# Attention and routed experts on one core: whole value tiles, scores on 64x32 tiles, sums from the exponentials, one comparison per rank block

## The chip, the cores and the metric

The kernel runs on 1 NeuronCore of one Trainium2 chip. The metric is the device time of one execution in microseconds (us), the median of several runs. The engines are TensorE (PE; its weight loads are PEld in the profile), VectorE (DVE), ScalarE (ACT), GpSimd (POOL) and SyncE (SP, which here only issues DMAs), and the core has 16 DMA engines. Each engine takes its instructions in program order and waits on semaphores.

## What is computed

Eight batches, 8 heads, 512 local and 32 global tokens, head size 64, all in fp32. A local query sees the 32 global keys and the local keys within 32 positions; a global query sees all 544 keys. Over the result, seen as 544 tokens of 512 numbers, a router takes the 128 tokens with the highest score in each batch, and these pass through two dense layers with a gate.

```python
k_all = np.concatenate([k_g, k_l], axis=2)
v_all = np.concatenate([v_g, v_l], axis=2)
out_g = np.matmul(sm(scale * np.matmul(q_g, k_all.transpose(0, 1, 3, 2))), v_all)
mask = np.abs(pos[:, None] - pos[None, :]) <= 32
s_ll = np.where(mask, scale * np.matmul(q_l, k_l.transpose(0, 1, 3, 2)), -1e9)
s_lg = scale * np.matmul(q_l, k_g.transpose(0, 1, 3, 2))
out_l = np.matmul(sm(np.concatenate([s_lg, s_ll], axis=-1)), np.concatenate([v_g, v_l], axis=2))
# sm(s): e = exp(s - max(s)); e / (sum(e) + 1e-9)
...
scores = np.einsum('bsd,d->bs', x, w_gate)          # x: tokens, 544 x 512
top_idx = np.argpartition(-scores[b], 128)[:128]
ye = np.maximum(x[b, top_idx] @ w1, 0.0) @ w2       # 512 -> 1024 -> 512
out[b, top_idx] = x[b, top_idx] + sigmoid(scores[b, top_idx])[:, None] * ye
```

## The kernel before

**Steps.** The attention runs in 64 steps: batch b, half of the heads hq (4 heads), and a quarter t of the local queries (128 queries). Four steps make a group, eight a batch. One loop writes the program order of PE, DVE, ACT and POOL by hand: iteration i issues the scores of step i+2, the products with the values of step i-1, the transposes of step i, the softmax of step i+1 and the normalising of step i-1. The order of DMA issues on SyncE is left to the framework.

**Scores.** `scores` computes for 32 queries of one chunk the products with their window of 128 keys (chunk before, own chunk, globals, chunk after; the keys lie in `k_t` in such an order that a window is one access pattern). Two heads share 128 partitions (64 numbers each), so `spread_q` writes the queries into `qbd` with zeros in the other head's half: a stationary operand of 128x64 gives both heads at once. A step is 8 such products into one PSUM bank `s_ps` of two. Each fp32 product is two matmul records in the trace, a transpose one.

**Softmax.** For each 128x128 block, four a step, VectorE adds the mask and takes the negated maximum (L238), and ScalarE takes the exponential in place (L242). PE transposes the four blocks (L250), ScalarE copies them out (`turned`, L255). `attend_mm` (L273) multiplies by the value tile `v_t`, whose rows have a 65th column of ones, so that the sum of the exponentials comes out as a 65th column. `attend_out` takes that sum, its reciprocal and scales (L284, L286, L291), once each step.

**Value tiles.** A group needs two (`half` 0 and 1). A tile holds 8 windows of 128 rows; rows 64 to 95 are the globals in each. `load_v` (L150) loads partitions 0 to 63 and 96 to 127 in two DMAs, and `fill_v` (L157) copies the globals from `vg_t` into partitions 64 to 95 on POOL. There are three buffers.

**Globals.** Once a group the `g_` functions do the same for the 32 global queries of 4 heads over all 544 keys, in the two banks `big`.

**Tokens to experts.** `finish` writes a step's 128 tokens to HBM and scores them (L302). When a batch is done, `chain` runs its links over the following steps: `spread` turns the 544 scores into a row on all partitions, `rank` (five times) counts for a block of 128 tokens how many tokens go before each, `onehot` compares the ranks with 0 to 127, `gather` turns that into indices on PE and fetches the tokens by an indirect DMA. Ties go by position: `rank` compares with `>=` over the tokens up to the own block (L406) and with `>` over the rest (L408), with weights `side_w` that cut the own block in a triangle. The experts' work of earlier batches (`ffn1_pair` L520, `ffn2` L536) is cut into pieces and put between the steps by `run_fill`; batches go in the groups (0), (1,2), (3,4), (5,6), (7). Its result goes back by an indirect DMA (L543).

Of the kernel before, what the change touches and what calls it, by code (L numbers as in the profile page):

```python
# [72 lines left out]
def kernel(ctx, tc, qT, kT, qgT, vw, vgw, w1, w2, wg, const, outs, cap):  # L73
# [24 lines left out]
    half = cst.tile([P, 2], FP32, name="half")  # L98
    nc.vector.memset(half, 0.0)
    for i in range(2):  # L100
        nc.vector.memset(half[D * i:D * i + D, i:i + 1], 1.0)
# [2 lines left out]
    nc.scalar.activation(out=warm, in_=half, func=AF.Exp)
    # Weights of a comparison by position: 0 and 1 at the tokens' own block, 1 in all blocks on the side that counts.
    side_w = cst.tile([P, SL + 2 * P], FP32, name="side_w")
    nc.gpsimd.memset(side_w[:, P:P + SL], 1.0)
# [3 lines left out]

    qbd = [cst.tile([P, 2, NC, 2, 32], FP32, name=f"qbd{i}") for i in range(2)]

    def load(b, hq):
# [4 lines left out]
        if b == 0 and hq == 0:  # L119
            nc.sync.dma_start(out=q_t[:, :, 0:P], in_=qT[b, :, prs, 0:P])  # L120
            nc.sync.dma_start(out=k_t[:, :, 0:2 * P], in_=kT[b, :, prs, 0:2 * P])
            nc.sync.dma_start(out=cs[:, 0:3 * P], in_=const[:, 0:3 * P])
            nc.sync.dma_start(out=q_t[:, :, P:SL], in_=qT[b, :, prs, P:SL])
            nc.sync.dma_start(out=k_t[:, :, 2 * P:KW], in_=kT[b, :, prs, 2 * P:KW])
        else:
            nc.sync.dma_start(out=q_t, in_=qT[b, :, prs])
            nc.sync.dma_start(out=k_t, in_=kT[b, :, prs])
# [734 lines left out]
```

## Time and profile before

| | us |
|---|---|
| median of 3 runs | 355.31 |
| lowest and highest | 353.08, 362.15 |
| span of the profiled execution, first to last instruction | 353.1 |

The page gives no other time for the profiled execution than its span; the lowest of the three runs lies beside it. In the prediction's rows, "busy" is the time in which an engine executed something, "xN" the number of instructions, "idle before" the time the engine stood still just before them, followed by what ended it. Rows in order of time begin with the start and the length in us. PEclk is the granted clock as a share of full speed, "DMA share" the busy share of the 16 DMA engines. L-numbers are lines of the kernel before.

### The profile page before, as it was taken

How to read it: one execution, taken by the hardware profiler on the slowest of the kernel's cores; microseconds unless marked ns; L12 is line 12 of the kernel's file. 1: busy time of each engine (PE TensorE's matmuls, PEld its weight loads, DVE VectorE, ACT ScalarE, POOL GpSimd, SP SyncE). 2: the span in 40 equal slices, each digit the busy share in tenths (PEclk: the TensorE clock that was granted, in tenths of full speed). 3: DMA queues.
4: the chain of work that ended last, by engine and by line, in shares of the span. 5: the costliest groups of instructions: out<-in, count | busy, mean ns of one | idle time of the engine just before them, and what ended most of it. 6: DMA issues, size and time to landing. Idle time of an engine off the chain costs nothing.

```text
span 353.1 us, 12662 instructions
## 1 busy us (share of the span) xinstructions
PE 307.8 (87%) x5112; PEld 244.1 (69%) x5112; DVE 261.5 (74%) x1142; ACT 172.0 (49%) x445; POOL 137.7 (39%) x91
## 2 busy tenths in 40 slices
PE   6766798678996969679899999999899999999993
PEld 2654576466674757467688887768698877699882
DVE  1334767898669996997689977998699799995222
ACT  2455737457662645245653663455655445322020
POOL 1326647708754633404395205154356112211111
PEclk9899889989999889969999999999999999999999
DMA  7999989987998593938986777659784841311000
GB/s 201 257 208 320 264 275 300 279 247 218 319 248 291 123 299 71 253 121 219 274 183 219 193 226 193 187 169 255 230 229 141 218 96 62 135 58 32 30 30 30
DMA packets 23033, 67.99 MB, mean 193 GB/s; under 512 B 7360, under 2 KB 9280, under 8 KB 19904
## 3 DMA queue, kind: packets, MB, share of 16 engines
q1 hardware_dynamic: 21696, 63.00, 63.9%
q0 software_dynamic: 1280, 4.20, 3.9%
q8 instruction: 40, 0.66, 0.8%
q14 instruction: 17, 0.14, 0.1%
HBM read 56.18 MB, written 11.01 MB: 190 GB/s over the span
## 4 chain that ended last, share of the span: by engine, by line
PE 35%; DVE 19%; issue 12%; POOL 3%; DMA 3%; ACT 1%; POOLq 0%; DVEq 0%; ACTq 0%; SPq 0%
PE s_ps L222 7%; PE m_ps L520 5%; DVE junk L406 5%; PE o_ps L273 4%; PE m_ps L536 4%; PE t_ps L250 4%; DVE p_t L238 3%; DVE junk L302 3%; DVE junk L408 2%; PE big L361 2%; PE big L318 2%; DVE x L291 1%; DMA xe<-out_dram,ix 1%; POOL qbd L145 1%; DMA xg<-out_dram 1%
## 5 line engine op out<-in xcount | busy, mean ns | idle before, releaser
L242 ACT ACTIVATE p_t<-p_t,nb 128x128 f32<-128x128 f32 x256 | 81.9, 393 | 77.4 <-DVE nb L238 77.2
L222 PE MATMUL s_ps<-k_t,qbd 128*64 128x128 f32 x1024 | 77.0, 296 | 27.2 <-issue 12.8
L222 PEld LDWEIGHTS s_ps<-k_t,qbd 128*64 128x64 f32 x1024 | 60.4, 147 | 42.8 <-issue 19.2
L157 POOL TENSOR_SCALAR v_t<-vg_t 32x2080 f32<-32x2080 f32 x32 | 65.1, 2035 | 54.5 <-issue 16.5
L238 DVE CUSTOM_DVE_ANT_0 p_t<-s_ps,cs 128x128 f32<-128x128 f32 x256 | 58.5, 284 | 3.2 <-PE s_ps L222 3.2
L273 PE MATMUL o_ps<-v_t,pt 128*32 128x65 f32 x2048 | 45.9, 229 | 7.1 <-issue 4.5
L255 ACT COPY pt<-t_ps 128x512 f32<-128x512 f32 x64 | 36.7, 574 | 25.5 <-PE t_ps L250 25.1
L273 PEld LDWEIGHTS o_ps<-v_t,pt 128*32 128x32 f32 x2048 | 34.5, 113 | 18.3 <-issue 13.0
L250 PE MATMUL t_ps<-cs,p_t 128*128 128x128 f32 x256 | 44.2, 298 | 0.0
L145 POOL TENSOR_SCALAR qbd<-q_t,half 128x1024 f32<-128x1024 f32 x29 | 34.6, 1201 | 14.5 <-DMA q_t<-in_qT_dram 8.7
L438 POOL DMA_INDIRECT xe<-out_dram,ix x8 | 8.7, 1087 | 69.1 <-issue 49.1
L406 DVE SCALAR_TENSOR_TENSOR junk<-r,sc,side_w 128x128 f32<-128x128 f32 (+4 forms) x40 | 34.7, 868 | 1.0 <-ACT r L394 0.3
L250 PEld LDWEIGHTS t_ps<-cs,p_t 128*128 128x128 f32 x256 | 28.2, 146 | 6.0 <-issue 0.9
L302 DVE CUSTOM_DVE_ANT_0 junk<-x,wgb 128x512 f32<-128x512 f32 x32 | 29.2, 913 | 0.8
L408 DVE SCALAR_TENSOR_TENSOR junk<-r,sc,side_w 128x544 f32<-128x544 f32 (+4 forms) x40 | 28.1, 704 | 1.6
L291 DVE TENSOR_TENSOR x<-o_ps,rec 128x256 f32<-128x256 f32 x64 | 27.2, 424 | 2.2
L284 DVE TENSOR_SCALAR den<-o_ps 128x4 f32<-128x4 f32 x64 | 10.0, 157 | 21.9 <-PE o_ps L273 13.1
L543 POOL DMA_INDIRECT out_dram<-xe,ix x8 | 8.2, 1023 | 36.1 <-DVE xe L541 28.8
L520 PE MATMUL m_ps<-xTh,w1h 128*128 128x256 f32 x80 | 21.2, 297 | 0.0
L238 DVE DVE_READ_ACCUMULATOR2_ANT nb<- 128x1 f32 x256 | 20.8, 81 | 0.0
L536 PE MATMUL m_ps<-w2h,hTh 128*128 128x512 f32 x48 | 20.7, 431 | 0.0
L520 PE MATMUL m_ps<-xTh,w1l 128*128 128x256 f32 x80 | 19.9, 282 | 0.0
(133 smaller groups left out, 485.0 us busy)
## 6 DMA issues: line engine op xcount, KB each, us to landing
v_t<-in_vw_dram SPq DMA_DIRECT2D x32, 520.0 KB
k_t<-in_kT_dram SPq DMA_DIRECT2D x15, 832.0 KB
v_t<-in_vw_dram SPq DMA_DIRECT2D x32, 260.0 KB
out_dram<-x SPq DMA_DIRECT2D x32, 256.0 KB
q_t<-in_qT_dram SPq DMA_DIRECT2D x15, 512.0 KB
ws<-in_w_dram SPq DMA_DIRECT2D x8, 512.0 KB
k_t<-in_kT_dram SPq DMA_DIRECT2D x1, 576.0 KB
vg_t<-in_vgw_dram SPq DMA_DIRECT2D x16, 32.5 KB
```

The lines of the kernel that those rows point to most:

```text
L145: nc.gpsimd.tensor_scalar(out=out, in0=in_, scalar1=h, scalar2=0.0, op0=ALU.mult, op1=ALU.add)
L157: nc.gpsimd.tensor_scalar(out=v_t[64:96], in0=bass.AP(tensor=src.tensor, offset=src.offset, ap=[src.ap[0], [0, 8], [1, 4 * VD]]), scalar1= ...
L222: nc.tensor.matmul(out=s_ps[D * par:D * par + D, pr, uu, :], lhsT=z[:, pr, c].rearrange("p a k -> p (a k)"), rhs=window(k_t[:, pr, k0:k0 + ...
L238: nc.vector.tensor_tensor_reduce(out=p_t[:, pr, uu, :], in0=s_ps[:, pr, uu, :], in1=m, op0=ALU.add, op1=ALU.min, scale=-0.125, scalar=BIG, ...
L242: nc.scalar.activation(out=p_t[:, pr, uu, :], in_=p_t[:, pr, uu, :], func=AF.Exp, scale=-1.0, bias=nb[:, pr, uu:uu + 1])
L250: nc.tensor.transpose(t_ps[:, pr, uu, :], p_t[:, pr, uu, :], ident)
L255: nc.scalar.copy(out=pt, in_=t_ps)
L273: nc.tensor.matmul(out=o_ps[32 * j:32 * j + 32, 2 * pr + h, :], lhsT=pt[:, pr, j // 2, x0:x0 + 32], rhs=v_t[:, j % 2, 2 * (t % 2) + j // 2 ...
L302: nc.vector.tensor_tensor_reduce(out=junk[:n, 0:DM], in0=xf, in1=wgb[:n], op0=ALU.mult, op1=ALU.add, scale=1.0, scalar=0.0, accum_out=dst,)
L406: nc.vector.scalar_tensor_tensor(out=junk[:n, 0:hi], in0=r[:n, 0:hi], scalar=s, in1=side_w[:n, P + SL - lo:P + SL - lo + hi], op0=ALU.is_g ...
L408: nc.vector.scalar_tensor_tensor(out=junk[:n, lo:ST], in0=r[:n, lo:ST], scalar=s, in1=side_w[:n, 0:ST - lo], op0=ALU.is_gt, op1=ALU.mult, ...
L520: nc.tensor.matmul(out=h_ps, lhsT=a[:, kc, ms], rhs=xT[x_][:, kc, :], start=(i == 0), stop=(i == len(prods) - 1))
```

## The change

- **Values**: `v_t` has 64 columns in place of 65, and one DMA of 128 partitions loads it whole, with the globals already in place in HBM. `fill_v`, `vg_t` and their 32 KB loads are gone.
- **Scores**: no `spread_q` and no `qbd`. Each head's 64 rows are contracted alone: stationary operand 64x32, tiles of the array 64 rows by 32 columns, 16 products a step in place of 8. Two steps are computed together into two banks, one for each row half, single-buffered, and issued at the end of every even iteration behind the experts' work. A block of the softmax is now one head by 128 queries.
- **Sums**: ScalarE's exponential also writes the sum of its row (`accum_out`); the column of ones is gone. `attend_out` runs once for two steps over 512 columns, except for the last two steps. The tiles `x` hold two steps, and `finish` comes up to a step later.
- **Globals**: the queries are scaled by 0.125 on POOL at each load, the maximum is negated in the reduction, and the sums come from the exponentials.
- **Ranks**: one comparison over all 544 tokens, `(r - s) > ahead`, where `ahead` is minus the smallest normal fp32 number for tokens that go first on a tie, and 0 otherwise. `onehot` is five comparisons of 128x128. The small transpose of `spread` goes to a bank of `m_tile`.

```diff
-    ps_s = ctx.enter_context(tc.tile_pool(name="ps_s", bufs=2, space=PSUM))
+    ps_s = ctx.enter_context(tc.tile_pool(name="ps_s", bufs=1, space=PSUM))
...
+    ahead = cst.tile([P, SL + ST], FP32, name="ahead")
+    nc.gpsimd.memset(ahead[:, 0:SL], -TINY)
+    nc.gpsimd.memset(ahead[:, SL + P:], 0.0)
...
+            k1 = 32 * (_wpos(3) + 5)
-            nc.sync.dma_start(out=k_t[:, :, 0:2 * P], in_=kT[b, :, prs, 0:2 * P])
+            nc.sync.dma_start(out=k_t[:, :, 0:k1], in_=kT[b, :, prs, 0:k1])
...
-        vg_t = ld.tile([P, 4, VD], FP32, name="vg_t")
-        nc.sync.dma_start(out=vg_t[64:96], in_=vgw[b, hq])
+        qgs = ld.tile([P, 2, SG], FP32, name="qgs")
+        nc.gpsimd.tensor_scalar(out=qgs, in0=qg_t, scalar1=0.125, scalar2=0.0, op0=ALU.mult, op1=ALU.add)
...
     def load_v(b, hq, half):
-        v_t = vld.tile([P, 2, 4, 4, VD], FP32, name="v_t")
-        for r0, r1 in ((0, 64), (96, 128)):
-            nc.sync.dma_start(out=v_t[r0:r1], in_=vw[b, hq, half, r0:r1])
+        v_t = vld.tile([P, 2, 4, 4, D], FP32, name="v_t")
+        nc.sync.dma_start(out=v_t, in_=vw[b, hq, half])
...
+    def scores(p):
+        b, hq, t = work[2 * p]
+        q_t, k_t = loaded[b, hq][:2]
+        banks = [ps_s.tile([P, 512], FP32, name=f"s{r}").rearrange("p (s h k) -> p s h k", s=2, h=2) for r in range(2)]
+        for s in range(2):
+            for pr in range(2):
+                for j in range(4):
+                    for r in range(2):
+                        c = 4 * (t + s) + j
+                        rows = slice(D * r, D * r + D)
+                        k0 = 32 * _wpos(c)
+                        nc.tensor.matmul(
+                            out=banks[r][32 * j:32 * j + 32, s, pr, :],
+                            lhsT=q_t[rows, pr, 32 * c:32 * c + 32],
+                            rhs=window(k_t[rows, pr, k0:k0 + P], c % 2),
+                            start=True, stop=True,
+                        )
+        return banks
...
+        for h in range(4):
+            nc.vector.tensor_tensor_reduce(
+                out=p_t[:, h, :], in0=banks[h % 2][:, s, h // 2, :], in1=m, op0=ALU.add, op1=ALU.min,
+                scale=-0.125, scalar=BIG, accum_out=nb[:, h:h + 1],
+            )
+            nc.scalar.activation(out=p_t[:, h, :], in_=p_t[:, h, :], func=AF.Exp,
+                                 scale=-1.0, bias=nb[:, h:h + 1], accum_out=dens[p][:, s, h])
...
+    def attend_mm(i, pt):
+        b, hq, t = work[i]
+        p, s = divmod(i, 2)
+        if s == 0:
+            O[p] = ps_o.tile([P, 2, 4, D], FP32, name="o_ps")
...
+    def attend_out(p, s0, s1):
+        b, hq, t = work[2 * p]
+        n = s1 - s0
+        den = sm.tile([P, 2, 4, 1], FP32, name="den")
+        nc.vector.tensor_scalar(out=den[:, s0:s1], in0=dens[p][:, s0:s1], scalar1=1e-9, scalar2=None, op0=ALU.add)
+        rec = sm.tile([P, 2, 4, 1], FP32, name="rec")
+        nc.vector.reciprocal(out=rec[:, s0:s1], in_=den[:, s0:s1])
...
+        nc.vector.tensor_tensor(out=xt[b, t][:, s0:s1, 4 * hq:4 * hq + 4, :], in0=O[p][:, s0:s1],
+                                in1=rec[:, s0:s1].broadcast_to([P, n, 4, D]), op=ALU.mult)
...
-        nc.vector.scalar_tensor_tensor(out=junk[:n, 0:hi], in0=r[:n, 0:hi], scalar=s, in1=side_w[:n, P + SL - lo:P + SL - lo + hi],
-                                       op0=ALU.is_ge, op1=ALU.mult, accum_out=cnt[:n, i, 0:1])
-        nc.vector.scalar_tensor_tensor(out=junk[:n, lo:ST], in0=r[:n, lo:ST], scalar=s, in1=side_w[:n, 0:ST - lo],
-                                       op0=ALU.is_gt, op1=ALU.mult, accum_out=cnt[:n, i, 1:2])
+        nc.vector.scalar_tensor_tensor(out=junk[:n], in0=r[:n], scalar=sc[b][0:n, i:i + 1], in1=ahead[:n, SL - lo:SL - lo + ST],
+                                       op0=ALU.subtract, op1=ALU.is_gt, accum_out=cnt[:n, i:i + 1])
...
-            at((b + 1) * per_b - NT + t + 1, finish, b, t)
+            at(min((b + 1) * per_b - NT + t - t % 2 + 2 + t % 2, nstep), finish, b, t)
...
-        if i + 2 < nstep:
-            S[i + 2] = scores(work[i + 2])
         if g is not None and t == 0:
             gst["big"] = g_scores(b, hq)
         if i > 0:
-            o_ps = attend_mm(work[i - 1], PT.pop(i - 1))
+            attend_mm(i - 1, PT.pop(i - 1))
...
-        if i > 0:
-            attend_out(work[i - 1], o_ps)
+        if i >= nstep - 1:
+            attend_out((i - 1) // 2, (i - 1) % 2, (i - 1) % 2 + 1)
+        elif i > 0 and i % 2 == 0:
+            attend_out(i // 2 - 1, 0, 2)
...
                 run_fill(max(0.0, min((have - LEFT) / (nstep - i), FILL)))
+        if i % 2 == 0 and i + 2 < nstep:
+            S[i // 2 + 1] = scores(i // 2 + 1)
```

More of the change, by code (lines that the diff above doesn't have):

```diff
@@ L90 @@
     ps_m = ctx.enter_context(tc.tile_pool(name="ps_m", bufs=2, space=PSUM))
-    cs = cst.tile([P, const.shape[1] - 2 * P], FP32, name="cs")
+    cs = cst.tile([P, const.shape[1] - P], FP32, name="cs")
     o = 0
@@ L97 @@
     tokid = cs[:, o:o + NT + 1]; o += NT + 1
[L98 to L101, printed above, removed]
     warm = cst.tile([P, 2], FP32, name="warm")
[L104 to L107 removed]
+    nc.vector.memset(warm, 0.0)
+    nc.scalar.activation(out=warm, in_=warm, func=AF.Exp)
+    ahead = cst.tile([P, SL + ST], FP32, name="ahead")
+    nc.gpsimd.memset(ahead[:, 0:SL], -TINY)
+    nc.gpsimd.memset(ahead[:, SL + P:], 0.0)
     wgb = cst.tile([P, DM], FP32, name="wgb")
     loaded = {}
[L112 removed]
     def load(b, hq):
@@ L210, in window @@
         return bass.AP(tensor=kk.tensor, offset=kk.offset, ap=[kk.ap[0], [32, 2], [64, 2], [1, 32]])
-    def scores(g):
-        b, hq, t = g
-        k_t = loaded[b, hq][1]
-        z = qbd[(NQ * b + hq) % 2]
-        s_ps = ps_s.tile([P, 2, 2, P], FP32, name="s_ps")
-        for pr in range(2):
-            for uu in range(2):
-                for par in range(2):
-                    c = 4 * t + 2 * uu + par
-                    k0 = 32 * _wpos(c)
-                    nc.tensor.matmul(
-                        out=s_ps[D * par:D * par + D, pr, uu, :],
-                        lhsT=z[:, pr, c].rearrange("p a k -> p (a k)"),
-                        rhs=window(k_t[:, pr, k0:k0 + P], par),
-                        start=True, stop=True,
-                    )
-        return s_ps
@@ L244, in softmax @@
         return p_t
     def transp(p_t):
-        t_ps = ps_t.tile([P, 2, 2, P], FP32, name="t_ps")
-        for pr in range(2):
-            for uu in range(2):
-                nc.tensor.transpose(t_ps[:, pr, uu, :], p_t[:, pr, uu, :], ident)
+        t_ps = ps_t.tile([P, 512], FP32, name="t_ps")
+        for h in range(4):
+            nc.tensor.transpose(t_ps[:, P * h:P * h + P], p_t[:, h, :], ident)
         return t_ps
     def turned(t_ps):
-        pt = att.tile([P, 2, 2, P], FP32, name="pt")
+        pt = att.tile([P, 4, P], FP32, name="pt")
@@ L281, in attend_out @@
-    def attend_out(g, o_ps):
-        b, hq, t = g
-        den = sm.tile([P, 4, 1], FP32, name="den")
-        nc.vector.tensor_scalar(out=den, in0=o_ps[:, :, D:VD], scalar1=1e-9, scalar2=None, op0=ALU.add)
-        rec = sm.tile([P, 4, 1], FP32, name="rec")
-        nc.vector.reciprocal(out=rec, in_=den)
+    O = {}
+    def attend_mm(i, pt):
+        b, hq, t = work[i]
+        p, s = divmod(i, 2)
+        if s == 0:
+            O[p] = ps_o.tile([P, 2, 4, D], FP32, name="o_ps")
+        v_t = loaded[b, hq][3][t // 2]
+        for h in range(4):
+            for j in range(4):
+                nc.tensor.matmul(
+                    out=O[p][32 * j:32 * j + 32, s, h, :],
+                    lhsT=pt[:, h, 32 * j:32 * j + 32],
+                    rhs=v_t[:, j % 2, 2 * (t % 2) + j // 2, h, :],
+                    start=True, stop=True,
+                )
@@ L366, in g_attend, with g_out @@
                 )
-    def g_out(b, hq, big):
-        og = big[:, 800:800 + VD]
-        den = sm.tile([P, 1], FP32, name="deng")
-        nc.vector.tensor_scalar(out=den, in0=og[:, D:VD], scalar1=1e-9, scalar2=None, op0=ALU.add)
+    def g_out(b, hq, big, deng):
+        og = big[:, 800:800 + D]
+        den = sm.tile([P, 1], FP32, name="dens_g")
+        nc.vector.scalar_tensor_tensor(out=den, in0=deng[:, 0:1], scalar=1e-9, in1=deng[:, 1:2], op0=ALU.add, op1=ALU.add)
         rec = sm.tile([P, 1], FP32, name="recg")
@@ L398, in spread @@
         rk[b] = (r, cnt)
+        oh[b] = moe.tile([P, NT + 1, NST * P], FP16, name="oh")
+    oh = {}
     def rank(b, i):
```

157 lines of the change are left out of this document (43 added, 114 removed).

## Prediction

> **What bounds the kernel now.** I read the busy shares of the page first, then the busy time in four stages whose borders I chose where the bound changes, then the groups by shape, then the order of time.
>
> ```profile
> span 353.1 us, 12662 instructions
> PE 307.8 (87%) x5112; PEld 244.1 (69%) x5112; DVE 261.5 (74%) x1142; ACT 172.0 (49%) x445; POOL 137.7 (39%) x91
> ```
>
> The shares name no single bound. The stages do:
>
> ```profile
> core 0: us, PE busy (x) PEld busy (x) DVE busy (x) ACT busy (x) POOL busy (x), PEclk, DMA share, GB/s
> 0.00:100.00 100.00, 77.72 (x1487) 57.97 (x1487) 62.06 (x314) 55.96 (x138) 52.23 (x35) 0.93 0.95 264
> 100.00:160.00 60.00, 48.51 (x842) 37.92 (x843) 53.06 (x213) 29.73 (x76) 23.98 (x13) 0.89 0.68 191
> 160.00:305.00 145.00, 139.47 (x2523) 112.27 (x2519) 123.69 (x549) 77.02 (x209) 55.19 (x37) 1.00 0.69 190
> 305.00:353.00 48.00, 42.11 (x274) 35.98 (x272) 22.65 (x69) 9.34 (x23) 6.30 (x7) 0.99 0.15 51
> ```
>
> Stage A (0 to 100) is DMA: 0.95 of the 16 engines. Stage B (100 to 160) is VectorE: 53.06 of 60 us, with PE at 48.51 and a granted clock of 0.89. Stage C (160 to 305) is PE: 139.47 of 145. Stage D is the tail behind the attention, PE with the experts' work: 42.11 of 48. So an edit is worth something in C only if it takes PE time, in B only if it takes VectorE time, in A only if it takes DMA time.
>
> **Stage A: the value tiles.** A value tile comes today in two DMAs of 64 and 32 partitions (520 and 260 KB), and POOL copies the other 32. After the change it is one DMA of 128 partitions, 1024 KB. More bytes in the stage that DMA bounds would be a loss, if all bytes cost the same. They don't (two rows of the DMA queue's order of time, three windows that I laid around such transfers, with DMA share and GB/s last, and the tile's row up to 97 us):
>
> ```profile
> 212.78 5.62 SPq L150 DMA_DIRECT2D v_t<-in_vw_dram  x4
> 224.89 0.41 SPq L127 DMA_DIRECT2D k_t<-in_kT_dram  x1
> 64.50:69.10 4.60, 3.88 (x101) 2.83 (x92) 3.86 (x10) 2.05 (x6) 4.51 (x4) 1.00 0.98 231
> 214.10:222.20 8.10, 8.10 (x133) 5.86 (x132) 5.95 (x20) 2.71 (x8) 4.15 (x3) 1.00 0.91 223
> 228.00:230.50 2.50, 2.40 (x68) 1.93 (x72) 2.33 (x9) 1.69 (x4) 0.85 (x1) 1.00 0.98 393
> L150 SPq DMA_DIRECT2D v_t<-in_vw_dram x22: 311/502/1303, 4.7 to 86.2; - x22
> ```
>
> In the two windows where value pieces fill the queue it moves 223 and 231 GB/s at shares of 0.91 and 0.98, so about 240 at a full share. Where the 128-partition k_t lands it moves 393 at 0.98, so 401. A tile costs 0.80 MB / 240 GB/s = 3.3 us now. Whole it costs 1.05 MB / 401 = 2.6 us if it runs like k_t (I take this: same partitions, one row per partition, rows of 8 KB beside 6.5), and 1.05 / 240 = 4.4 us if value rows are slow for another reason. 22 issues, 11 tiles, fall in stage A: 11 x (2.6 - 3.3) = **-8 us**; the other end is 11 x 1.1 = +12. The 32 KB vg_t loads go too; I count nothing for them, nor for SyncE, which issues 2 value DMAs a group of 4 steps in place of 5 (502 ns the median).
>
> The row above shows slow pieces, not why. [...]
>
> **Stage B: VectorE.** Four edits take VectorE time (six groups with busy us and mean ns, then five rows from the order of time).
>
> ```profile
> L406 DVE SCALAR_TENSOR_TENSOR junk<-r,sc,side_w 128x128 f32<-128x128 f32 (+4 forms) x40 | 34.7, 868 | 1.0 <-ACT r L394 0.3
> L408 DVE SCALAR_TENSOR_TENSOR junk<-r,sc,side_w 128x544 f32<-128x544 f32 (+4 forms) x40 | 28.1, 704 | 1.6
> L302 DVE CUSTOM_DVE_ANT_0 junk<-x,wgb 128x512 f32<-128x512 f32 x32 | 29.2, 913 | 0.8
> L291 DVE TENSOR_TENSOR x<-o_ps,rec 128x256 f32<-128x256 f32 x64 | 27.2, 424 | 2.2
> L284 DVE TENSOR_SCALAR den<-o_ps 128x4 f32<-128x4 f32 x64 | 10.0, 157 | 21.9 <-PE o_ps L273 13.1
> L286 DVE RECIPROCAL rec<-den 128x4 f32<-128x4 f32 x64 | 11.4, 178 | 2.2
> 68.38 2.13 POOL L157 TENSOR_SCALAR v_t<-vg_t 32x2080 f32<-32x2080 f32 x1
> 68.77 2.14 DVE L406 SCALAR_TENSOR_TENSOR junk<-r,sc,side_w 128x384 f32<-128x384 f32 x1
> 314.65 0.61 DVE L406 SCALAR_TENSOR_TENSOR junk<-r,sc,side_w 128x384 f32<-128x384 f32 x1
> 311.79 0.78 DVE L408 SCALAR_TENSOR_TENSOR junk<-r,sc,side_w 128x544 f32<-128x544 f32 x1
> 306.27 0.69 DVE L302 CUSTOM_DVE_ANT_0 junk<-xe,wgb 128x512 f32<-128x512 f32 x1
> ```
>
> Ranks: 40 pairs (34.7 + 28.1 = 62.8 us) become 40 single comparisons over 544 elements. The undisturbed 544 form takes 0.78: 31 us, so -32. Part of that is relief: the same 128x384 comparison takes 0.61 us alone and 2.14 beside POOL's value copy. Scores of the tokens (L302) have two SBUF inputs as well: 0.913 mean, 0.69 undisturbed, 32 x 0.22 = -7. POOL's copies and spreads (L157, L145) end, and what they waited for goes with them; POOL keeps the weights' splits, the indirect DMAs and a new 128x64 scaling for qgs at each load, which waits for its DMA with the gathers queued behind it. Normalising: 64 x (0.157 + 0.178 + 0.424) = 48.6 us becomes 32 x (0.157 + 0.178 + 0.69), the last by the 256-element row plus as much per element again: 33, so -16. g_max loses one small operation 16 times: -2. The one-hot in five pieces I put equal. Together -57 of 261.5, or 22%. In stage B that is 53.06 - 11.6 = 41.5 us, so PE is late next: 48.51 less the scores (11.5 steps x 0.44, below) = 43.5, plus some 5.5 us of idle that I keep: 49 us, **-11**.
>
> **Stage C: the scores on PE.**
>
> ```profile
> 202.61 1.09 PE L222 MATMUL s_ps<-k_t,qbd 128*64 128x128 f32 x16
> 203.63 0.67 PE L273 MATMUL o_ps<-v_t,pt 128*32 128x65 f32 x32
> 204.23 0.65 PE L250 MATMUL t_ps<-cs,p_t 128*128 128x128 f32 x4
> 195.31 1.12 PE L318 MATMUL big<-k_t,qg_t 64*32 64x512 f32 x16
> 196.36 0.67 PE L273 MATMUL o_ps<-v_t,pt 128*32 128x65 f32 x32
> 160.00:305.00 145.00, 32.64 (x478) 25.18 (x473) 1.00 0.69 190
> ```
>
> From start to next start a step's scores take 203.63 - 202.61 = 1.02 us: 16 records of 128 columns, 64 ns each with two column tiles in flight. After the change there are 32 records a step on 64x32 tiles, eight in flight. Lower bound by the four-tile product: 0.60 us for 32 records is 19 ns each, though with 65 columns. By L318, also 64x32 and four in flight: 8 records of 512 and 8 of 32 columns in 1.05 us, so a tile spends 1.05 on 1088 columns and four weight loads; a 128-column record is about 142 ns, over eight tiles 18 ns. The other end is no gain (32 ns). I take 18: 0.58 a step, -0.44. The last row is the window of stage C for line 222 alone, 478 records, 30 steps: 30 x 0.44 = **-13 us**. In A the same gain is under the DMA. VectorE at 123.69 x 0.78 = 96 of 132 and DMA at 0.69 are not late next.
>
> [...] The trace has 19 ns in o_ps, so I go by the row.
>
> **What is added.** Each exponential now also writes its sum. No row shows that on ScalarE; VectorE's own read of its sum and ScalarE's smallest instruction are nearest:
>
> ```profile
> L238 DVE CUSTOM_DVE_ANT_0 p_t<-s_ps,cs 128x128 f32<-128x128 f32 x256 | 58.5, 284 | 3.2 <-PE s_ps L222 3.2
> L238 DVE DVE_READ_ACCUMULATOR2_ANT nb<- 128x1 f32 x256 | 20.8, 81 | 0.0
> L470 ACT ACTIVATE ge<-ss 128x1 f32<-128x1 f32 x8 | 1.6, 203 | 21.4 <-DVE ss L302 21.4
> 201.48 1.28 ACT L242 ACTIVATE p_t<-p_t,nb 128x128 f32<-128x128 f32 x4 [2.02 <-DVE nb L238]
> 202.67 0.56 ACT L255 COPY pt<-t_ps 128x512 f32<-128x512 f32 x1
> 270.74 2.10 DMA out_dram<-ogs
> 272.91 4.50 DMA xg<-out_dram
> PE s_ps L222 <- DMA k_t<-in_kT_dram: 5.5, 2, 3.8
> ```
>
> Nothing if it rides along, 0.20 x 4 = 0.8 us a step at most; I take 0.15 each, 0.6 a step. ScalarE goes from 172 to some 210 us of 325. It is hidden as long as the four exponentials and the turn (1.28 + 0.6 + 0.56 = 2.4 us) fit beside a step, and stage C's 132 us over 30 steps are 4.4. The scores of a pair of steps stand at the end of the even step, behind the experts' work, and wait until VectorE has read the odd step's; behind them wait the next step's products. VectorE reads those at the head of its step, one step before, so I count nothing. The first scores now cover two steps and may wait for the second piece of k_t, as later ones do today (3.8 us the longest): 0 to +4, and I take 0, since the DMA sets stage A and doesn't pause for it. The tokens' outputs leave a step later, and steps get shorter, while ogs to HBM and xg back (2.10 + 4.50 us) do not: I add 0.6 us for each of 7 batches, **+4**. In D five pairs of comparisons become five, under PE's experts: **-1**.
>
> Sum: -8 - 11 - 13 - 1 + 4 = -29 on 353.1, 324 us. The runs' median of 355.31 lies 2.2 above that span and their lowest, 353.08, on it; I put the median of the changed kernel at **325 us**.
>
> **Rivals.**
> 1. ScalarE's sums come on the path. For: turned(i) stands behind the exponentials of step i+1 on its queue. Against: ScalarE has 68 idle us in stage C. If half the steps wait 0.5 us: +16, 341.
> 2. The bytes count and value rows stay at 240 GB/s. Against: the k_t window. +12 for -8 in stage A: 345.
> 3. The scores don't do what they should, and 32 records take as long as 16. For: no row has eight tiles. Against: 19 ns in o_ps. 41 steps in B and C x 0.44 = 18: 343.
> 4. Slower: the pair's scores, single in their banks, make a ring. From their end come the first maximum (0.284 + 0.081 = 0.36), four exponentials at up to 0.5 with their sums (2.0) and the turn (0.56), 2.9 us, before the product that opens PE's next even step; what covers it without experts' work is one product and one transpose, 1.2. That leaves 1.7 us in each of 32 pairs, 54, less 29: 378. It decides from 0.9 us a pair. Against it: experts' work fills most steps from stage B on, and in A the DMA sets 92 us for 23 steps, 4 each.
>
> **How the numbers follow.** Forecast, 310 to 335: 0.60. Rival 1: 0.14. Rival 2: 0.08. Rival 3: 0.07. Rival 4: 0.06. Faster than 310, if stage A's gaps close too: 0.05. A change within 2% (348.2 to 362.4), which is about what a measurement here cannot tell from none, gets 0.06 from the upper parts of 1 to 3. Faster 0.88, slower 0.06. The range takes in rivals 1 to 3 and leaves out rival 4, what lies under 308 and the mixtures of rivals above 346: 308 to 346.
>
> **What would show it.** Right: windows of v_t near 390 GB/s; scores' records under 0.65 us a step; the 544 comparison near 0.78 us and no 128x512 score above 0.8; PE over 0.9 busy from about 90 us on. Wrong: waits of PE's scores for VectorE's maxima, or of the products for the turn, longer than the
>
> ```profile
> PE s_ps L222 <- DVE nb L238: 8.1, 5, 4.2
> ```
>
> us in all that stand there now; v_t windows still near 230 GB/s; ScalarE busy beyond 230 us. The forecast fails if one of these rings closes in most steps, since every gain here is under half a microsecond a step.

## The result and the profile after

The changed kernel takes 336.05 us, the median of 4 runs, against 358.21 us for the kernel before on the same chip. One of these 4 took 340.92 us at a granted clock of 0.946, the others 334.87 to 336.66 at 0.959 to 0.971, and the ratios of this document leave such slower executions out on both sides: here 0.948, with an interval of 0.942 to 0.954, faster by 5.2%, where the two medians over all runs give 0.938. The profiled execution has a span of 333.6 us, 19.5 less than before.

First the head of the page, then five stretches of the span whose borders I put at the transposes that open steps 0, 20, 32 and 63, so that each stretch holds the same work in every kernel of this document. The columns are those of the stage table in the prediction: stretch, length, busy us of PE, PEld, DVE, ACT and POOL, granted clock, DMA share, GB/s.

```profile
span 333.6 us, 14662 instructions
PE 277.9 (83%) x6136; PEld 216.8 (65%) x6136; DVE 211.6 (63%) x964; ACT 194.1 (58%) x731; POOL 43.0 (13%) x55
```

```profile
0.00:11.90 11.90, 7.50 (x89) 3.32 (x89) 2.02 (x17) 2.83 (x9) 1.82 (x8) 1.00 0.80 275
11.90:97.30 85.40, 59.23 (x1740) 43.60 (x1736) 54.40 (x249) 59.60 (x226) 16.86 (x15) 0.96 0.85 306
97.30:147.90 50.60, 43.04 (x1090) 32.69 (x1086) 37.04 (x177) 35.41 (x132) 8.19 (x8) 0.93 0.76 264
147.90:284.30 136.40, 125.37 (x2957) 100.89 (x2952) 96.63 (x462) 86.88 (x342) 10.48 (x18) 0.97 0.64 223
284.30:333.60 49.30, 42.78 (x284) 36.34 (x276) 21.51 (x62) 9.33 (x23) 5.67 (x7) 0.98 0.13 49
```

The kernel before, by the same steps (steps 0 to 20, 20 to 32, 32 to 63):

```profile
15.40:100.20 84.80, 67.83 (x1424) 51.73 (x1416) 58.80 (x291) 51.06 (x127) 49.12 (x28) 0.94 0.97 273
100.20:162.30 62.10, 50.60 (x896) 39.21 (x894) 53.47 (x215) 30.59 (x78) 26.17 (x16) 0.89 0.69 191
162.30:304.50 142.20, 136.66 (x2460) 110.38 (x2456) 122.69 (x545) 76.16 (x206) 52.51 (x35) 1.00 0.69 191
```

The reader is to see where the 19.5 us came from: 3.5 before step 0, nothing in stage A (84.8 to 85.4), 11.5 in stage B, 5.8 in stage C, and -0.7 in the tail. Every engine has less to do in total except ScalarE, yet in stage A TensorE has 8.6 us less work and the stage is no shorter: its idle time grew from 17.0 to 26.2 us.

The groups of the changed kernel that answer to the priced edits (busy us, mean ns, then idle before them):

```profile
L224 ACT ACTIVATE p_t<-p_t,nb 128x128 f32<-128x128 f32 x256 | 99.6, 392 | 67.0 <-DVE nb L220 66.7
L200 PE MATMUL s<-k_t,q_t 64*32 64x128 f32 x2048 | 41.8, 289 | 13.3 <-DVE nb L220 8.4
L224 ACT ACTIVATION_READ_ACCUMULATOR p_t<-p_t,nb 128x1 f32 x256 | 48.2, 188 | 0.0
L386 DVE SCALAR_TENSOR_TENSOR junk<-r,sc,ahead 128x544 f32<-128x544 f32 (+1 forms) x40 | 32.4, 810 | 1.5 <-POOL cnt L366 0.6
L268 DVE TENSOR_TENSOR x<-o_ps,rec 128x512 f32<-128x512 f32 (+1 forms) x33 | 22.3, 676 | 9.4 <-PE o_ps L250 4.9
L279 DVE CUSTOM_DVE_ANT_0 junk<-x,wgb 128x512 f32<-128x512 f32 x32 | 25.1, 785 | 0.5
```

Scores fell from 77.0 us on TensorE (the group of L222 before, below) to 41.8; the ranks are one comparison of 0.81 us; the product that normalises two steps takes 0.68. Then the waits (total, times, longest), the rows of the kernel before that answer to them, and a piece of the chain of waits in stage C, in order of time:

```profile
DVE junk L279 <- DMA xg<-out_dram: 18.2, 7, 4.9
PE o_ps L250 <- ACT pt L236: 11.6, 12, 2.6
PE s L200 <- DVE nb L220: 8.4, 4, 3.0
```

```profile
L222 PE MATMUL s_ps<-k_t,qbd 128*64 128x128 f32 x1024 | 77.0, 296 | 27.2 <-issue 12.8 <-DVE nb L238 8.1 <-DMA k_t<-in_kT_dram 5.5
DVE junk L302 <- DMA xg<-out_dram: 2.5, 4, 1.1
PE o_ps L273 <- ACT pt L255: 1.6, 2, 0.8
```

```profile
247.04 0.29 DVE ogs L352
247.36 4.44 DMA out_dram<-ogs
251.82 6.40 DMA xg<-out_dram
258.27 0.08 issue
258.35 0.68 DVE junk L279
...
267.08 1.09 PE s L200 x64
```

The first wait was 2.5 us before. Here VectorE stands at the score of the globals until 258.35 (4.9 us, the longest of the seven waits), and the next step's maxima run behind it, from 259.31 on. The two transfers took 10.8 us where the pair quoted in the prediction took 6.6.

### The profile page after: what moved, and what is told of

It reads as the page before. It is cut to its first block, busy times and chain, and to the rows that moved or that the text cites. A ratio compares the mean times of both kernels' runs of the same rounds, so it can differ in the third digit from the quotient of the medians.

```text
span 333.6 us, 14662 instructions
## 1 busy us (share of the span) xinstructions
PE 277.9 (83%) x6136; PEld 216.8 (65%) x6136; DVE 211.6 (63%) x964; ACT 194.1 (58%) x731; POOL 43.0 (13%) x55
## 4 chain that ended last, share of the span: by engine, by line
PE 37%; DMA 23%; issue 17%; DVE 9%; ACT 8%; SPq 2%; POOL 2%; POOLq 0%; DVEq 0%; ACTq 0%
DMA xg<-out_dram 9%; DMA out_dram<-ogs 7%; PE s L200 7%; PE o_ps L250 6%; PE t_ps L231 6%; DMA qg_t<-in_qgT_dram 6%; ACT p_t L224 5%; PE m_ps L508 4%; PE big L295 3%; PE big L338 3%; PE m_ps L492 3%; DVE p_t L220 2%; DMA k_t<-in_kT_dram 2%; PE big L323 2%; ACT pt L236 2%
## 5 line engine op out<-in xcount | busy, mean ns | idle before, releaser
L224 ACT ACTIVATE p_t<-p_t,nb 128x128 f32<-128x128 f32 x256 | 99.6, 392 | 67.0 <-DVE nb L220 66.7
L220 DVE CUSTOM_DVE_ANT_0 p_t<-s,cs 128x128 f32<-128x128 f32 x256 | 58.7, 284 | 22.0 <-PE s L200 19.7
L250 PE MATMUL o_ps<-v_t,pt 128*32 128x64 f32 x2048 | 45.5, 230 | 22.7 <-ACT pt L236 11.6
L200 PE MATMUL s<-k_t,q_t 64*32 64x128 f32 x2048 | 41.8, 289 | 13.3 <-DVE nb L220 8.4
L224 ACT ACTIVATION_READ_ACCUMULATOR p_t<-p_t,nb 128x1 f32 x256 | 48.2, 188 | 0.0
L200 PEld LDWEIGHTS s<-k_t,q_t 64*32 64x32 f32 x2048 | 31.3, 111 | 23.1 <-issue 9.7
L386 DVE SCALAR_TENSOR_TENSOR junk<-r,sc,ahead 128x544 f32<-128x544 f32 (+1 forms) x40 | 32.4, 810 | 1.5 <-POOL cnt L366 0.6
L268 DVE TENSOR_TENSOR x<-o_ps,rec 128x512 f32<-128x512 f32 (+1 forms) x33 | 22.3, 676 | 9.4 <-PE o_ps L250 4.9
L295 PE MATMUL big<-k_t,qgs 64*32 64x512 f32 (+1 forms) x256 | 20.0, 412 | 5.2 <-DVE nb L220 2.4
L492 PE MATMUL m_ps<-xTh,w1h 128*128 128x256 f32 x72 | 19.7, 306 | 3.1 <-DVE hTl L495 3.1
L279 DVE CUSTOM_DVE_ANT_0 junk<-xg,wgb 32x512 f32<-32x512 f32 x8 | 8.8, 1098 | 18.3 <-DMA xg<-out_dram 18.2
L508 PE MATMUL m_ps<-w2l,hTh 128*128 128x512 f32 x48 | 19.4, 405 | 0.0
```

Of the source, the lines that this page charges most:

```text
L200: nc.tensor.matmul(out=banks[r][32 * j:32 * j + 32, s, pr, :], lhsT=q_t[rows, pr, 32 * c:32 * c + 32], rhs=window(k_t[rows, pr, k0:k0 + P] ...
L220: nc.vector.tensor_tensor_reduce(out=p_t[:, h, :], in0=banks[h % 2][:, s, h // 2, :], in1=m, op0=ALU.add, op1=ALU.min, scale=-0.125, scala ...
L224: nc.scalar.activation(out=p_t[:, h, :], in_=p_t[:, h, :], func=AF.Exp, scale=-1.0, bias=nb[:, h:h + 1], accum_out=dens[p][:, s, h])
L250: nc.tensor.matmul(out=O[p][32 * j:32 * j + 32, s, h, :], lhsT=pt[:, h, 32 * j:32 * j + 32], rhs=v_t[:, j % 2, 2 * (t % 2) + j // 2, h, :] ...
L268: nc.vector.tensor_tensor(out=xt[b, t][:, s0:s1, 4 * hq:4 * hq + 4, :], in0=O[p][:, s0:s1], in1=rec[:, s0:s1].broadcast_to([P, n, 4, D]), ...
L279: nc.vector.tensor_tensor_reduce(out=junk[:n, 0:DM], in0=xf, in1=wgb[:n], op0=ALU.mult, op1=ALU.add, scale=1.0, scalar=0.0, accum_out=dst,)
```

## Experiments

Each stands beside a run of the kernel before on the same chip; times are medians of all runs, and ratios are to that kernel. The experiments did not all run on one chip, and the kernel before took 353.1 to 358.2 us beside them, so a difference of some 4 us between two of them is not sure by its size alone. An edit starts from the changed kernel where its heading names no other.

**Value tile in two halves** (same bytes, same 8 KB rows):

```diff
-        nc.sync.dma_start(out=v_t, in_=vw[b, hq, half])
+        for r0 in (0, 64):
+            nc.sync.dma_start(out=v_t[r0:r0 + 64], in_=vw[b, hq, half, r0:r0 + 64])
```

> Changed kernel with each value tile loaded in two DMAs of 64 partitions, same bytes, same rows of 8 KB. Theory (partitions: half a tile moves at half the rate, as the 223 to 231 GB/s of the kernel before): the tile goes from 2.9 to about 4.4 us, the first stage gets 11 x 1.5 = 16 us longer, and the time rises by 10 to 20 us. Rival (length of rows or number of DMAs sets the rate, not the partitions; two DMAs after each other on one queue overlap): the tile stays near 2.9 us and the time within 3 us.

371.71 us, ratio 1.049 [1.026, 1.071]: the whole gain of the change is gone and more. Steps 0 to 20:

```profile
13.00:115.20 102.20, 68.84 (x1738) 50.53 (x1736) 51.48 (x249) 59.92 (x226) 16.81 (x15) 0.83 0.94 257
```

16.8 us longer than 85.4, as the theory had it; at full share all transfers of the stage together moved 257 / 0.94 = 273 GB/s against 306 / 0.85 = 360. What I did not expect is the rest: stage B is 6.0 us longer and stage C 13.6, so that (371.71 - 336.05) / 32 tiles is 1.1 us for a tile in the mean of the run. Part of it lies in TensorE's own records, which took longer: the same work was 68.84 us in place of 59.23 in A and 131.82 in place of 125.37 in C, at a granted clock of 0.83 in place of 0.96 and 0.95 in place of 0.97.

The edit changes two things, the partitions of a DMA and its size (512 KB in place of 1 MB). The traces tell them apart. A row of a value tile, a packet of 8192 bytes, took 309 ns in the median when the tile came whole and 590 in halves. The loads of queries and weights, also 512 KB but over all 128 partitions in packets of 4096 bytes, took 159 and 167 ns a packet in the same two runs. So DMAs of 512 KB are not slow as such, and of the two the partitions are left. The kernel before agrees: its rows of 8320 bytes, in DMAs of 64 and 32 partitions, took 585 ns in the median. Why a row takes longer there, no run shows. A packet takes 1.9 times as long; all transfers of the stage together lose a quarter of their rate.

**Whole value tiles alone, on the kernel before** (one DMA of 128 partitions with the 65th column in its rows; `fill_v`, `vg_t` and its load gone):

```diff
-        for r0, r1 in ((0, 64), (96, 128)):
-            nc.sync.dma_start(out=v_t[r0:r1], in_=vw[b, hq, half, r0:r1])
+        nc.sync.dma_start(out=v_t, in_=vw[b, hq, half])
```

> Kernel before with whole value tiles alone: one DMA of 128 partitions (rows of 8320 bytes, with the column of ones), no copy on GpSimd, no small global load. Theory (partitions set the rate): 11 tiles in the first stage at some 3.0 us in place of 3.44, so 4 to 6 us less by step 20; VectorE no longer runs beside GpSimd's copies and stage B loses another 3 to 5: 7 to 11 us less than before in all, 344 to 348. Rival (a third more bytes for the same queue, the copies were hidden): no gain or a loss of up to 10 us by step 20 and none later.

334.33 us against 354.01, more than either theory gave, and as much as the whole change. Steps 0 to 20, 20 to 32, 32 to 63:

```profile
13.90:88.60 74.70, 64.59 (x1423) 49.79 (x1415) 58.65 (x291) 51.06 (x127) 27.78 (x18) 0.95 0.92 339
88.60:138.50 49.90, 45.53 (x902) 34.90 (x894) 45.01 (x215) 30.25 (x78) 12.49 (x9) 1.00 0.82 290
138.50:284.90 146.40, 138.39 (x2462) 111.77 (x2456) 115.73 (x545) 76.80 (x206) 22.16 (x21) 0.98 0.59 203
```

Stage A is 10.1 us shorter and stage B 12.2, with the same 291 and 215 VectorE instructions. In B these take 45.01 us in place of 53.47. This is relief from GpSimd's copies (26.17 us of GpSimd there before, 12.49 now). In both traces every comparison and every score of tokens that ran over 0.1 us longer than the shortest of its shape ran beside a GpSimd instruction. The surplus of these in stage B is 10.7 us before and 2.2 here, and the difference is the 8.5 us by which VectorE's time fell. The first comparison of the ranks, before and here (duration in ns: lowest, median, highest):

```profile
L406 DVE SCALAR_TENSOR_TENSOR junk<-r,sc,side_w x40: 341/752/2280, 62.4 to 317.5; 128x128 f32<-128x128 f32 x8, 128x256 f32<-128x256 f32 x8, 128x384 f32<-128x384 f32 x8, 128x512 f32<-128x512 f32 x8
L394 DVE SCALAR_TENSOR_TENSOR junk<-r,sc,side_w x40: 341/619/1483, 53.2 to 297.6; 128x128 f32<-128x128 f32 x8, 128x256 f32<-128x256 f32 x8, 128x384 f32<-128x384 f32 x8, 128x512 f32<-128x512 f32 x8
```

The surplus stands only beside GpSimd's instructions; by what the two hinder each other, no run shows. GpSimd still spreads the queries in this kernel, and the longest comparison still takes 1483 ns in place of 2280.

Of the 12.2 us, 7.1 are less idle time of TensorE (4.4 in place of 11.5 us); the other 5.1 are its own work, 45.53 us in place of 50.60 at a granted clock of 1.00 in place of 0.89, and the last section shows that the clock itself follows such idle time. Stage C, with its new wait for the globals' rows (14.5 us over the run, 2.5 before), became 4.2 us longer.

**The single rank comparison added to that** (with the one-hot in five pieces):

```diff
-        nc.vector.scalar_tensor_tensor(out=junk[:n, 0:hi], in0=r[:n, 0:hi], scalar=s, in1=side_w[:n, P + SL - lo:P + SL - lo + hi],
-                                       op0=ALU.is_ge, op1=ALU.mult, accum_out=cnt[:n, i, 0:1])
...
+        nc.vector.scalar_tensor_tensor(out=junk[:n], in0=r[:n], scalar=sc[b][0:n, i:i + 1], in1=ahead[:n, SL - lo:SL - lo + ST],
+                                       op0=ALU.subtract, op1=ALU.is_gt, accum_out=cnt[:n, i:i + 1])
```

> Kernel before with whole value tiles (334.3 us) and the single comparison per rank block with the one-hot in five pieces. Theory: VectorE loses about 25 us of 246, but no stage is bound by VectorE any more once GpSimd's copies are gone (45 of 50 us in stage B, PE 45.5): 0 to 4 us less, 330 to 334. The prediction's reading (VectorE bounds stage B) would give 5 to 8 us less between steps 20 and 32. Rival: five one-hot pieces add latency between the last rank and the gather, 0 to 2 us more.

334.12 us, ratio 0.943 [0.935, 0.950], against 334.33 without it: no difference that can be measured. VectorE's total fell from 245.6 to 229.5 us. In this one profile stage B is 3.1 us shorter, below the 5 to 8 of the prediction's reading. Stages B and C:

```profile
90.50:137.30 46.80, 45.46 (x898) 34.97 (x894) 40.80 (x201) 30.27 (x78) 13.22 (x9) 1.00 0.87 307
137.30:280.70 143.40, 136.25 (x2459) 110.28 (x2457) 106.41 (x517) 77.22 (x206) 22.51 (x21) 1.00 0.60 208
```

What the comparison is worth without whole tiles was not measured.

**The chain one step later, the score of the globals at its head** (from the changed kernel):

```diff
-START = (1, 1, 1, 1, 1, 1, 0)
+START = (2, 2, 2, 2, 2, 2, 1)
```

> Changed kernel with every batch's chain, the score of its globals first, one step later. Theory: what is missing of the forecast is VectorE standing at the head of each chain for the globals' rows on their way to HBM and back (18.2 us in 7 waits), and a step more (about 4.3 us) hides most of it: the wait falls under 4 us in all, and the time falls by 6 to 12 us, to 324 to 330. Rival (the wait only takes the place of idle time that TensorE's order or the granted clock would leave anyway): the wait goes and the time stays within 2 us of 336.

331.66 us, ratio 0.943 [0.931, 0.954], 4.4 less than the changed kernel and short of the 6 to 12 of the theory; the intervals of the two ratios overlap, but on the same chip the next two experiments took 336.48 and 335.52. The wait for xg is gone from the list altogether. Steps 32 to 63 and the tail:

```profile
147.70:275.30 127.60, 119.35 (x2943) 95.53 (x2935) 95.38 (x459) 88.56 (x349) 9.06 (x17) 1.00 0.67 238
275.30:329.80 54.50, 47.51 (x303) 39.99 (x299) 24.09 (x73) 9.32 (x24) 7.42 (x8) 0.99 0.14 46
```

Stage C lost 8.8 us, and the tail gained 5.2: the whole chain moved, so that experts' work came ready a step later and was left for the tail (47.51 us of TensorE there, 42.78 before the edit).

**Four value buffers** in place of three:

```diff
-    vld = ctx.enter_context(tc.tile_pool(name="vld", bufs=3))
+    vld = ctx.enter_context(tc.tile_pool(name="vld", bufs=4))
```

> Changed kernel with four buffers for the value tiles in place of three. Theory: with three, SyncE stands for a buffer that the globals' products free (73.9 us in 12 waits), the store of the globals' result stands behind it on SyncE's queue and then behind the 1 MB tile on the DMA engines; with four the load goes out a group earlier, the round trip shrinks from 10.8 to about 7 us and the time falls by 4 to 8 us. In the first 97 us, where the DMA engines set the pace, nothing changes. Rival (the bytes ahead of the round trip are the same whenever they are issued): the wait of VectorE for the globals' rows stays above 14 us and the time within 2 us.

336.48 us, ratio 0.957 [0.944, 0.969]: nothing. The wait for xg went from 18.2 to 13.9 us, and the time does not show it. SyncE's standing for a buffer did not set the pace.

**Exponentials without their sums** (`accum_out` left out, and the denominators the constant 40, which GpSimd writes):

```diff
+            nc.gpsimd.memset(dens[p], 40.0)
...
-                                 scale=-1.0, bias=nb[:, h:h + 1], accum_out=dens[p][:, s, h])
+                                 scale=-1.0, bias=nb[:, h:h + 1])
```

> Changed kernel whose exponentials do not write their sums; the denominators are the constant 40, so the sums are left out of the computation. Theory: the read of the sum, 0.188 us after each of 256 exponentials, lengthens their pitch by only 0.09 and lies beside TensorE's work: ScalarE falls from 194 to about 172 us and the time by 0 to 4 us. Rival 1 of the prediction (the turn behind the exponentials is on the path): the products' wait for the turn (11.6 us in 12 waits) goes to the 1.6 of before and the time falls by 8 to 16 us.

335.52 us, ratio 0.950 [0.935, 0.965]: no change. ScalarE fell from 194.1 to 171.6 us, as expected, and it was not on the path. The sums' price in the changed kernel is seen in ScalarE's order of time:

```profile
203.49 0.39 ACT L224 ACTIVATE p_t<-p_t,nb 128x128 f32<-128x128 f32 x1
203.78 0.19 ACT L224 ACTIVATION_READ_ACCUMULATOR p_t<-p_t,nb 128x1 f32 x1
203.87 0.39 ACT L224 ACTIVATE p_t<-p_t,nb 128x128 f32<-128x128 f32 x1
```

The read is 0.19 us long, but it begins while the exponential ends, and the next begins while the read ends: one exponential every 0.38 to 0.39 us. Before, four took 1.28 us in the row the prediction quotes; three intervals and one duration of 0.39 make that 0.30 us each. So a sum costs about 0.09, not 0.15; ScalarE's 22.5 us over 256 exponentials give the same.

**The globals' queries without GpSimd's scaling**:

```diff
-        nc.gpsimd.tensor_scalar(out=qgs, in0=qg_t, scalar1=0.125, scalar2=0.0, op0=ALU.mult, op1=ALU.add)
...
+        nc.vector.tensor_scalar(out=nb, in0=nb, scalar1=0.125, scalar2=None, op0=ALU.mult)
...
-                func=AF.Exp, bias=nb, accum_out=deng[:, part:part + 1])
+                func=AF.Exp, scale=0.125, bias=nb, accum_out=deng[:, part:part + 1])
```

> Changed kernel that takes the globals' queries as they are loaded, with the factor 0.125 in the exponential and one more small VectorE operation for the maximum, as the kernel before does; GpSimd's scaling is gone. Theory: the scaling itself is short (0.25 us) and the load in front of it late, but it stands on GpSimd's queue behind weight splits and ahead of the gathers, 16 times; without it steps 0 to 20 get 1 to 4 us shorter and the time 332 to 335. Rival (the load is late, not GpSimd): within 1.5 us. A larger gain, over 6 us, would make this the main loss in stage A.

335.81 us, ratio 0.951 [0.943, 0.959]: no change, as the rival had it; where GpSimd's 16 scalings stand does not set the time.

**Three buffers for queries and keys** in place of two:

```diff
-    ld = ctx.enter_context(tc.tile_pool(name="ld", bufs=2))
+    ld = ctx.enter_context(tc.tile_pool(name="ld", bufs=3))
```

> Changed kernel with three buffers for queries and keys in place of two. Theory: in the first 97 us the DMA engines are no longer full (share 0.84) and what sets the pace is the next group's load, released late and landing 9 us after its issue (21% of the chain there is qg_t); with a third buffer it goes out earlier, and steps 0 to 20 get 4 to 8 us shorter, steps after 20 stay within 2 us: 328 to 332. Rival (the queue's order sets it: the same bytes stand ahead whenever it is issued): steps 0 to 20 stay within 2 us and so does the time.

332.45 us, ratio 0.942 [0.936, 0.947], 3.6 less. Steps 0 to 20:

```profile
12.00:94.80 82.80, 62.62 (x1738) 46.19 (x1735) 52.05 (x249) 59.95 (x226) 17.30 (x15) 0.88 0.86 313
```

2.6 us less than 85.4: the direction is the theory's, the size less than the 4 to 8 it said. The same steps took 85.4 to 89.3 us in the profiles of the changed kernel and of the four edits above it that leave whole tiles and the buffers of queries and keys alone, so 82.8 lies outside their spread.

**Scores step by step**, at the head of every step and each in its own half of the two banks, in place of two steps at once at the end of an even step:

```diff
-        if i % 2 == 0 and i + 2 < nstep:
-            S[i // 2 + 1] = scores(i // 2 + 1)
+        if i + 2 < nstep:
+            scores(i + 2)
```

> Changed kernel with its scores on the same 64x32 tiles, but issued step by step at the head of the step, as the kernel before does, each step in its own half of the two banks; so a step's scores wait only for maxima read a step earlier. Theory now: whole value tiles alone gave all 20 us on the kernel before, so the rest of the change saves 22 us of TensorE and gives it back in waits; the largest is the pair of scores at the end of the even step, in single banks behind the experts' work (the fourth rival's ring in a mild form). Then steps 0 to 20 get 5 to 9 us shorter, steps 20 to 63 by 3 to 8, in all 320 to 328. Rival (the ring costs nothing; the globals' queries over GpSimd and the round trip of their rows do): within 2.5 us of 336.

331.58 us, ratio 0.939 [0.932, 0.946], 4.5 less: between the two expectations. On the same chip the edit of the globals' queries took 335.81. Steps 0 to 20 took 82.9 us (14.06 to 96.97), 2.5 us less, not 5 to 9. So the place of the pair's scores had a price, less than a tenth of the fourth rival's 54 us; whether it was the ring or their standing behind the experts' work, the edit doesn't separate, since it ends both.

**The pair's scores issued twice**:

```diff
-        for s in range(2):
+        for s in (0, 1, 0, 1):
```

> Changed kernel that issues the 64 records of a pair's scores twice over, so PE has 0.545 us more a step (32 x 1.09 us in all) and nothing else changes. Theory (as the forecast had it): up to step 20 the DMAs set the pace and it costs under 3 us; from there to the end of the attention TensorE does, and the 43 steps cost 43 x 0.545 = 23 us: 355 to 362. Rival (TensorE is no longer the bound after the change; waits between engines set the steps): it costs less than half of that from step 20 on, 336 to 348.

400.22 us, ratio 1.133 [1.122, 1.143], beyond both. The three stages, and the group of the scores:

```profile
12.60:116.70 104.10, 76.67 (x2377) 59.16 (x2376) 50.74 (x257) 61.25 (x230) 17.19 (x15) 0.84 0.70 252
116.70:175.90 59.20, 47.82 (x1473) 37.46 (x1469) 36.90 (x177) 35.45 (x132) 8.76 (x8) 0.94 0.65 225
175.90:347.80 171.90, 146.83 (x3920) 119.62 (x3912) 97.47 (x462) 88.36 (x342) 10.36 (x18) 0.94 0.52 176
```

```profile
L200 PE MATMUL s<-k_t,q_t 64*32 64x128 f32 x4096 | 72.2, 284 | 14.8 <-issue 11.4 <-DMA k_t<-in_kT_dram 3.4
```

30.4 us more of score records cost 64 us, 18.7 of them in stage A, where the DMA share was only 0.70. So after the change TensorE and what hangs on it set stage A as well. The span is 63.2 us longer: 30.4 are the added records, 13.7 the other records of TensorE, which took longer (mean granted clock 0.915 in place of 0.966), and 19.1 are idle time of TensorE. The expectation had "nothing else changes", and that does not hold: a step's half of the bank is written a second time before its first maximum, so VectorE waits longer too (19.7 us for the scores in the changed kernel, 58.9 here). The run therefore shows that stage A is not the DMA's alone; it is no clean price for TensorE time.

**The best of both sides.** The changed kernel with the three edits that helped, the globals' score moved without moving the rest of the chain; and the kernel before with whole tiles, the single comparison and the same move of the globals' score, its scores, sums and normalising left as they were:

```diff
-START = (1, 1, 1, 1, 1, 1, 0)
+START = (2, 2, 2, 2, 2, 2, 1)
...
     def chain(b):
         g_score(b)
-        yield
         while yp.get("open"):
```

> Changed kernel with the three edits that helped alone: scores step by step, the globals' score one step later (with the next link following at once, so that the ranks and the experts' work come no later and the tail does not grow), and three buffers for queries and keys. Theory (the 30 us that the change took from TensorE were given back in three kinds of waits, each of which one edit removes): the gains of -4.5, -4.4 and -3.6 us add up in part, 322 to 328. Rival (they cover the same idle time, and another wait takes its place): 329 to 332.

> Kernel before with whole value tiles, the single rank comparison and the globals' score one step later; scores, sums and normalising as before. The counterpart of the other run: its TensorE is 91% busy with 299 us of work, so it has little left to gain. Theory: the wait for the globals' rows (14.9 us) goes, TensorE's own work stays the bound: 328 to 333, and the other kernel, with 22 us less TensorE work, is at least 4 us faster. Rival (the work saved on TensorE is not worth anything even with the waits gone): the two are within 2 us of each other.

321.59 us, ratio 0.905 [0.895, 0.916], and 322.03 us, ratio 0.913 [0.906, 0.919]. Both are faster than the changed kernel's 0.948, and between the two no difference can be measured. (One of the six executions of the second took 926.4 us; the median hardly feels it.) That is the rival of the second text; its theory, 328 to 333 and at least 4 us slower than the other kernel, failed on both counts. Against the whole tiles with the single comparison (334.12 us, 0.943), the second differs by the move of the globals' score alone, and that took 12.1 us off, with intervals that don't touch: stage C went from 143.4 to 136.5, and the wait for the globals' rows, before and after the move, from 14.9 to 5.1:

```profile
DVE junk L291 <- DMA xg<-out_dram: 14.9, 6, 6.1
DVE junk L291 <- DMA xg<-out_dram: 5.1, 2, 2.8
```

Steps 0 to 20 and 32 to 63, of the first (whose profiled execution, 322.9 us, was its longest; the shortest took 315.8) and of the second:

```profile
14.40:95.40 81.00, 62.88 (x1738) 45.37 (x1735) 52.17 (x247) 57.79 (x215) 16.88 (x15) 0.85 0.84 304
144.10:272.10 128.00, 123.85 (x2925) 98.49 (x2920) 97.42 (x462) 88.18 (x347) 10.30 (x18) 0.99 0.67 232
```

```profile
15.20:90.00 74.80, 63.97 (x1422) 48.37 (x1415) 57.10 (x284) 50.99 (x127) 27.36 (x18) 0.98 0.91 329
136.60:273.10 136.50, 135.61 (x2465) 110.27 (x2457) 107.15 (x517) 77.88 (x206) 22.66 (x21) 1.00 0.65 223
```

In these two profiles the new scores, sums and normalising win 8.5 us in stage C and lose 6.2 in A, and 3.5 more in B (48.7 against 46.6) and in the tail (49.0 against 47.6). In A the granted clock was 0.85 against 0.98: TensorE's work took 62.88 us there, where the same work took 59.23 in the changed kernel at 0.96. The tail of the first is back at 49.0 us, so the move of the rest of the chain was what had filled it.

## Why the prediction was right, and where it was not

The time, 336.05, lies in the range and on the side that was forecast, 11 above the 325. But the sum came out by errors of both signs: whole value tiles alone are worth what the change is worth, and the terms for TensorE and VectorE together are worth nothing here. The 3.5 us won before step 0 stand in no term. That the total came near is in part luck.

| stage | kernel before | whole tiles alone | the change | forecast term |
|---|---|---|---|---|
| A, steps 0 to 20 | 84.8 | 74.7 | 85.4 | -8 |
| B, 20 to 32 | 62.1 | 49.9 | 50.6 | -11 |
| C, 32 to 63 | 142.2 | 146.4 | 136.4 | -13 |
| tail | 48.6 | 47.2 | 49.3 | -1 |

- **Value tiles, -8 in A.** Mechanism right, size about right: -10.1 where it stands alone. The step took a whole tile to run like k_t, and it does: 8192 bytes in 309 ns, beside k_t's 6656 in 253. So its second rival is refuted. But the step costed only 11 tiles in stage A, and "in C only if it takes PE time" hid that in the changed kernel a tile in halves costs 1.1 us in the mean of all stages.
- **Stage B, -11.** The number came out (-11.5), but mostly by another of the edits than the ones that the step added up. It put into one term fewer VectorE instructions and relief from GpSimd's copies; whole tiles alone give -12.2 there with the same instructions, and the single comparison then -3.1 in one profile and nothing in the time. The step that failed is "Part of that is relief", which was not priced by itself. VectorE's total fell by 50 us, of 57 forecast.
- **Scores, -13 in C.** The size was right. Line 200 alone in stage C of the changed kernel, and line 210, the same scores in the kernel with whole tiles alone:

```profile
147.90:284.30 136.40, 18.55 (x960) 14.24 (x960) 0.97 0.64 223
138.50:284.90 146.40, 32.35 (x464) 25.07 (x464) 0.98 0.59 203
```

 13.8 us less, and stage C 10.0 us shorter than with whole tiles alone. A pair takes 1.09 us for 64 records (the row at 267.08 of the chain), 17 ns each where 18 was taken. But against the kernel before, stage C is only 5.8 us shorter: whole tiles alone made it 4.2 longer.
- **What stage A lost, priced at nothing.** Here the prediction failed. "In A the same gain is under the DMA" kept the DMA as the bound; with whole tiles the queue isn't full (0.85), and A is set by chains between the engines, which the change made longer: +10.7 us against whole tiles alone, with 26.2 us of idle TensorE in place of 10.1. Of it, step-by-step scores give back 2.5 and a third buffer 2.6, each in one profile, and all three edits together 4.4. GpSimd's scaling, the sums and the value buffers give back nothing that can be measured. 6.2 us stay open, and so does which edit made the chains longer, since neither the new scores nor the shared normalising was tried alone on whole tiles. The granted clock isn't the cause of the 10.7: it was 0.96 there in the changed kernel and 0.95 with whole tiles alone.
- **The round trip, +4.** Right in mechanism, too small in size. Moving the whole chain took 4.4 us off the changed kernel, but filled its tail by 5.2; moving the score alone took 12.1 off the kernel with whole tiles and the single comparison. The wait was longer (18.2 us for 4), and whole tiles alone have it too (14.5 us); what was read as a cost of shorter steps may first be a cost of 1 MB transfers ahead of it on the queue, as the 10.8 us of the chain suggest; no run took those transfers away.
- **Sums, hidden.** Right: 0.09 us each, and nothing won without them. The first rival is refuted, though the products' wait for the turn grew from 1.6 to 11.6 us.
- **The ring, fourth rival.** At most 4.5 us of the 54 given for it; the forecast was right to leave it a small chance.
- **The signs.** Two of those named for "wrong" came, though the time lies in the range: the scores' wait for the maxima is 8.4 us and the products' wait for the turn 11.6, where 8.1 was the limit. Of those for "right", TensorE was over 0.9 busy in stage C (125.37 of 136.40 us) but not in B (43.04 of 50.60). Signs that stand for small terms do not judge a total.

## What to carry over

When one change does several things, price each with the others absent: here one edit, a value tile in one DMA over all partitions, was worth as much as all of them together, and more than half of that came in a stage where the DMA share had been only 0.69 and GpSimd no longer copied values beside VectorE. Work taken from a busy engine is worth what the next chain allows, so look at the stage after the bound has moved, and ask there what is in order behind what. A link that waits for a trip through memory should be moved alone, without the work that follows it.
